# Scans in three parts, pairwise state sums, merged early loads, halved projections and a new order in a two-branch kernel

## The chip, the cores and the metric

The kernel runs on one core of a Trainium2 chip. The metric is device microseconds of one execution. Its engines are TensorE (PE, with its weight loads shown as PEld), VectorE (DVE), ScalarE (ACT), GpSimd (POOL) and SyncE (SP), which issues nearly all DMAs. Each engine takes its instructions strictly in its own program order and waits on semaphores for the others.

## The reference

Two branches on 2048 positions of width 448, all in bf16, joined along the last axis.

```python
# A: attention with 16 heads of 28, each position sees itself and 7 earlier ones, 2 apart
qkv = x @ wqkv;  idx = pos - 2 * arange(8)
logits = einsum("bhsd,bhswd->bhsw", q, k[idx]) * 28 ** -0.5   # -1e9 where idx < 0
o = einsum("bhsw,bhswd->bhsd", softmax(logits), v[idx]);  a = o @ wo
# B: a diagonal complex state space model, 448 states
Lam_bar = exp(exp(log_dt) * Lam);  Bu = x @ (((Lam_bar - 1) / Lam)[:, None] * Bmat).T
h[t] = Lam_bar * h[t - 1] + Bu[t]
b = 2 * real(h @ Cmat.T) + x * Dskip
out = concatenate([a, b], axis=-1)
```

## The kernel before, in words

The program is a list of small steps. ORDER is a string of step names written out by hand or by a planner outside the kernel; the loop at the end calls each step once, in that order, and a step puts its instructions at the end of the queue of the engine that does them. So ORDER alone sets every engine's order, and nothing is rearranged afterwards. In a name such as `QK051`, `QK` is the step and 0, 5, 1 its arguments; `@31` gives the PSUM banks (of eight); a dot at the end makes an eviction an ACT instruction, `=` a DVE one. Steps in capitals are mostly TensorE's, those in small letters the evictions and elementwise work behind them.

**Head.** SP's queue starts with the loads of A's x (`xnA`), of parts of wqkv (`w_load`, 96 KB each in pieces of 128 columns, `w_half` for the last 64 rows), then A's second half, B's x and B. `WU` and `WF` are matmuls of zeros. `XI0`, `XI1`, `XI2` transpose x's first 512 positions on TensorE, `xi..` evict them, `XH1`, `XA10`, `XA11` with `xh1`, `xa..` do the next 512; positions 1024 to 2047 are transposed by DMA (line 183). `PP`, `pcopy`, `pa` to `pg` make the 448 decay rates and tables of constants; `ty`, `tk`, `tf`, `ts` make cosine and sine tables for groups of 64 states (7 groups). POOL fills constants, among them `iot` and `kph`, which `pe` reads.

**Attention.** `QS`(m, s) and `QK`(u, m, k) project q (m even) and k (m odd) of one half u, in four matmuls of 512 columns for the 448 rows of x: three of 128 rows and one of 64. In `QK` and in `V_` (values) and `BU` (B's projection) the 64-row matmuls of two blocks run side by side as one step with last argument 1 (line 259). `qk`, `qh`, `v` evict. `P`(u, r, ws) multiplies q with four shifted k on DVE (line 405, 2048 columns, one of 7 buffers), and `E_`(u, r) sums over the head's rows with matmuls of 32 columns (lines 417, 421); E_06 and E_16 are the last of each half. `lt` evicts logits, `TD` transposes them by DMA, `sma`, `smb`, `smc` are the softmax. `AL`, `al` spread the weights into bands in `Ak` (evictions that need Ak filled with zeros by POOL), `ad` writes them to DRAM and `sp` reads them back skewed into strips `PT` (line 529; PT is first filled with zeros by POOL, `pm0` to `pm2`, line 973; `pm4` fills Ak's second half in the tiles oT and ya, `pm3` wo). `AV`, `av` apply them to the values, `W_`, `w`, `ow` project and store.

**State space.** Time is split into chunks of T = 4 positions, and chunks into even (EV) and odd (OD). `BD` and `xt` are DMA transposes of B and x, `BU` projects, `BR` adds the rotated previous position (line 761), `z` evicts to Z (Z3 for the fourth). `UP` adds even chunks to the odd ones, `y` evicts; the scan runs over odd chunks only. `sa` rotates by table into a real scan, `sb` scans (one instruction a group), `sd` rotates back: in parts of two groups, 0, 2, 4, and group 6 alone, on three work tiles (vv, p2, hs). `DN`(g) and `dn`(g) give the even chunks' states, one group at a time. `H_`, `h` add states to position 0; for positions 1 and 2 `sw` swaps real and imaginary halves by DMA, `hp` multiplies on ACT and `hy`, `hz` add on DVE. `LC`, `ci`, `CD`, `ca`, `cs` load, transpose and scale C. `C`(j, ct), `c`, `oc` give the output, `CH`, `ch`, `oh` the last tile in halves.

`OZ` opens the tiles Z and Z3 in the space of the head's inputs, with a small fill on POOL (line 949) that waits for the last reader of that space, the transposes BD; `OP` opens PT, oT, wo and ya in the space of q, k and C. POOL's order is OZ, pm3, pm4, pm0, pm1, pm2. SP's order behind the head's loads is xt0, TD0, BD0, xt2, xt3, xt1, LC, BD1, TD1, LD, CD3, CD0, CD2, CD1, ad0, ad1, wo, sp0, sp1, ad2 and so on.

Of the kernel before, what the change touches and what calls it, by code (L numbers as in the profile page):

```python
# [63 lines left out]
def kernel(  # L64
# [169 lines left out]
    kph = const.tile([128, 2, 5, G], F32, tag="kph")  # L234
    for k in range(5):
        POOL.memset(kph[:, 0, k], max(k, 1) / (2.0 * T))
    POOL.memset(kph[:, 1], 0.0)
    POOL.memset(kph[64:128, 1, 1:5], 0.25)
# [777 lines left out]
```

## Time and profile before

| | |
|---|---|
| median of 3 executions | 127.11 us (126.85 to 127.17) |
| the profiled execution | 127.13 us |
| its span, first to last instruction | 125.4 us |
| granted TensorE clock | 1.00 |
| instructions | PE 1061, DVE 211, ACT 198, POOL 49 |

All numbers of the prediction come from the profiled execution; what lies around its span is 1.7 us. A row of the timeline has the start in us, the time from the first start to the last end, the engine, the line, the operation with what it writes and reads, the shape and the count, and in square brackets the idle time before it and what ended it. A matmul row is for TensorE, whose instructions overlap: one of 512 columns is shown some 0.38 us long, and the distance of starts tells what it costs. A row of a group has, after the bar, busy us and mean ns of one, then idle us before. A row of stretches has PE, PEld, DVE, ACT and POOL busy time with counts, then the clock, the DMA engines' busy share and GB/s.

### The profile page before, as it was taken

The numbers are of one execution on the slowest core, as the hardware profiler recorded it, in microseconds if no ns is written. First come the engines' busy times: TensorE is split into PE (matmuls) and PEld (weight loads), VectorE is DVE, ScalarE is ACT, GpSimd is POOL, SyncE is SP. The second block draws the span as 40 slices with busy tenths as digits, with TensorE's granted clock in tenths as the row PEclk, the third lists the DMA queues.
The fourth block names the chain that finished last, engine by engine and source line by source line (L and its number), as shares of the span: only waits on it lengthen the run. The fifth ranks groups of instructions, "written<-read, shape, count | busy, mean of one in ns | idle before, by whom it ended". The sixth has DMA issues, their size and how long they took to land.

```text
span 125.4 us, 2898 instructions
## 1 busy us (share of the span) xinstructions
PE 120.6 (96%) x1061; PEld 59.0 (47%) x1061; DVE 113.6 (91%) x211; ACT 102.4 (82%) x198; POOL 22.7 (18%) x49
## 2 busy tenths in 40 slices
PE   6999999999999999999999998999999999999990
...
DVE  4588999899999999999999999999999999998561
ACT  0599899897596999889999999999999999980000
...
GB/s 97 208 278 204 325 251 181 191 194 253 157 143 213 204 204 224 144 127 188 358 221 129 160 154 400 156 100 160 177 130 120 0 169 54 124 103 141 227 180 74
DMA packets 57493, 22.34 MB, mean 178 GB/s; under 512 B 43943, under 2 KB 56935, under 8 KB 57479
## 3 DMA queue, kind: packets, MB, share of 16 engines
...
q10 hardware_dynamic: 207, 0.07, 0.3%
...
## 4 chain that ended last, share of the span: by engine, by line
PE 77%; ACT 17%; DVE 2%; issue 2%; ACTq 0%; DVEq 0%
PE ps L259 27%; PE ps L897 16%; PE ps L573 10%; ACT Z L114 7%; ACT ctmp L722 5%; PE ps L417 5%; PE ps L374 4%; PE ps L560 4%; PE ps L277 2%; PE ps L827 1%; PE ps L375 1%; PE ps L922 1%; PE ps L761 1%; ACT L694 1%; PE ps L421 1%
## 5 line engine op out<-in xcount | busy, mean ns | idle before, releaser
L405 DVE TENSOR_TENSOR pr<-qf,kf 128x2048 bf16<-128x2048 bf16 x24 | 27.9, 1220 | 0.7 <-PE ps L417 0.4
L259 PE MATMUL ps<-xbuf,BT 128*128 128x512 bf16 (+1 forms) x112 | 25.1, 380 | 0.0
L897 PE MATMUL ps<-Cw,Z 128*128 128x448 bf16 x105 | 20.9, 352 | 0.0
L259 PE MATMUL ps<-xT,wq 128*128 128x512 bf16 (+1 forms) x72 | 16.0, 380 | 0.0
L259 PEld LDWEIGHTS <-BT 128*128 128x128 bf16 (+1 forms) x112 | 9.1, 96 | 12.9 <-issue 4.5
L897 PEld LDWEIGHTS <-Z 128*128 128x128 bf16 x105 | 10.3, 98 | 9.5 <-DVE Z L883 0.2
L114 ACT CAST Z<-ps 128x512 bf16<-128x512 f32 (+1 forms) x28 | 13.8, 547 | 0.2
L573 PE MATMUL ps<-wo,oT 128*128 128x448 bf16 x64 | 13.7, 353 | 0.0
L259 PE MATMUL ps<-wq,xT 128*128 128x448 bf16 (+1 forms) x64 | 12.3, 353 | 0.0
L973 POOL MEMSET PT<- 128x4320 f32 x3 | 11.0, 3698 | 4.7 <-DVE z L461 4.7
L259 PEld LDWEIGHTS <-wq 128*128 128x128 bf16 (+1 forms) x72 | 5.9, 97 | 8.6 <-issue 2.4
L722 ACT ACTIVATE ctmp<-Cw,c2t 64x448 f32<-64x448 bf16 x14 | 9.3, 666 | 0.2
L573 PEld LDWEIGHTS <-oT 128*128 128x128 bf16 x64 | 6.2, 98 | 5.7
L259 PEld LDWEIGHTS <-xT 128*128 128x128 bf16 (+1 forms) x64 | 5.2, 97 | 6.8 <-issue 2.4
L114 ACT CAST qf<-ps 128x512 bf16<-128x512 f32 x12 | 6.8, 594 | 1.8 <-PE ps L259 1.5
L114 ACT CAST oT<-ps 128x512 bf16<-128x512 f32 x15 | 8.1, 641 | 0.0
L114 ACT CAST v_s<-ps 128x448 bf16<-128x448 f32 x16 | 7.9, 548 | 0.0
L761 PE MATMUL ps<-Z,R 128*128 128x512 bf16 x21 | 7.3, 381 | 0.5 <-ACT Z L114 0.5
L114 ACT CAST kf<-ps 128x512 bf16<-128x512 f32 x12 | 7.1, 604 | 0.3 <-PE ps L375 0.2
L949 POOL MEMSET Z<- 128x14 bf16 x1 | 0.1, 111 | 38.9 <-ACT Cn L117 38.9
L374 PE MATMUL ps<-xT,wq 128*128 128x512 bf16 x24 | 6.6, 379 | 0.3 <-DVE u L627 0.2
L872 ACT ACTIVATE PT<-PT,bcol 128x512 bf16<-128x512 bf16 x8 | 6.3, 816 | 0.0
...
## 6 DMA issues: line engine op xcount, KB each, us to landing
PT<-pd SPq DMA_DIRECT2D x16, 156.0 KB, 4.8
...
```

Of the source, the lines that this page charges most:

```text
L114: (ACT.copy if e == "A" else V.tensor_copy)(o, i)
L259: PE.matmul(o, l, r, start=(first and i == 0), stop=(not first and i == len(pairs) - 1 and not more[s]))
L374: PE.matmul(p[:], wqk(m, slice(0, 128), kt), xT[:, 0, 4 * s + kt], start=(kt == 0), stop=False)
L405: V.tensor_tensor(t[:], q.unsqueeze(1).to_broadcast((128, 4, 512)), k4, ALU.mult)
L417: PE.matmul(acc[s][32 * i:32 * i + 32], E[:, f, ws, :], t[:, i, :], start=(f == 0 and ws == 0), stop=False)
L560: PE.matmul(p[32 * hh:32 * hh + 32, 128 * bl:128 * bl + n], v_s[:, t, 4 * hg + hh, :], PT[:, t % NS, (4 * hg + hh) // HS, (4 * hg + hh) % ...
L573: PE.matmul(p[:, 0:D], late["oT"][:, b // 4, hg, par, 128 * (b % 4):128 * (b % 4) + 128], late["wo"][:, hg, :], start=(hg == 0), stop=(hg ...
L722: ACT.activation(t[a:a + 64, 0:D], Cw[b:b + 64, g, :], ACTF.Copy, scale=c2t[a:a + 64, g:g + 1])
L761: PE.matmul(pp["z", g, j][:], rot(g, 0), late["Z"][:, g, j - 1, :], start=False, stop=True)
L872: ACT.activation(t, late["SW"][:, NC * g:NC * (g + 1)], ACTF.Copy, scale=bcol[:, j - 1, g:g + 1])
L897: PE.matmul(p[:, 0:D], z, Cw[:, g, :], start=(g == 0), stop=(g == G - 1))
L973: POOL.memset(late["PT"][:, 4 * i:4 * i + 4].rearrange("p t g n -> p (t g n)").bitcast(F32), 0.0)
```

## The change

The scans are done in parts of 2, 3 and 2 groups (0, 2 and 5) on two work tiles: the product that had its own tile goes into hs before the scan and into vv behind it. DN and dn treat groups 0 and 1, 2 and 3, 5 and 6 together in one bank, group 4 alone. The first 256 columns of q and of k are loaded by one DMA each (192 KB) in place of two. A step QA(m, a) projects half of a 512-position block, for m = 0 and 1, in place of QS00 and QS10. POOL fills kph ahead of iot. ORDER is new throughout: which engine evicts what (all four evictions of XI0 and XI1 are DVE's; tk2 to tk6 are ACT's, where all tk were DVE's), the place of every step, and with it the order of each queue. SP's is now LC, TD0, xt2, BD0, xt0, xt1, xt3, LD, CD2, CD0, CD3, TD1, CD1, BD1, ad1, ad0, wo, sp0, sp1, ad2; POOL's is OZ, pm3, pm0, pm1, pm4, pm2, with mz and ab ahead. BU300 stood ahead of E_16 and is now behind it.

```diff
-WU@0 XI0@1 WF0 xi00= xi01= XI2@2 PP@3 pcopy pa XI1@4 WF1 WF2 WF3 xi10. xi20= pb pd_ pc pe xi11. QS00@5 QS10@6 QS30@7
-XH1@0 ty0 ty1 pf tk0= tk1= tf0 XA10@1 xh1= QS20@3 pg ab rb0 ts00 xa10. XA11@2 xa11. QK050@40 qk000. xt0 qk010. P000
-qk020. QS11@1 qk011. P001 mz QS01@2 qk001. qk030. ts10 P010 ts20 ty4 QS21@5 QS31@6 qk031. qk021. QK041@31 tk4= QK051
-P011 V_101@27 QK040 V_100 wj. QK060@65 ty5 qk041. qk040. qk051. v101. V_000@13 qk050. V_011@07 QK061 V_001 v100.
-qh011. P020 E_00@42 v000. v001. P021 E_02 tk5= tf2 qh010. P030 qh001. qh000. E_01 P031 P040 P041 P050 P051 V_010
-V_400@13 hc0 P060 v011. v010. QK110@56 ts02 ts12 V_401 QK101@70 QK111 E_03 P061 qk110. qk111. QK100 qk100. QK120@56
-E_04 qk101. ts22 E_05 E_06 lt00 lt01 QK131@70 QK121 v401. qk120. TD0 QK130 qk130. v400. QK150@42 QK151 QK141@35
-QK161@71 qk131. qk150. P100 P101 P110 qk121. qk151. E_10@03 P111 P120 QK140 qk141. P121 QK160 qk140. V_110@46 V_501@25
-qh110. ty2 V_111 P130 P131 qh111. v110. qh101. qh100. v111. E_11 E_12 V_500 V_410@14 V_510@76 V_411 V_511 ty3 BD0 hc1
-sma0 smb0 E_13 P140 v500. v501. P141 P150 P151 E_14 E_15 v511. v510. xt2 xt3 xt1 BU300@25 v410. v411. P160 P161 LC
-E_16 lt11 BD1 lt10 TD1 smc0 OZ BU301 z30. ci1. LD BU001@67 BU101@14 BU000 ci3. z00. BR31 BU100 BU201@30 z10. AL0@2
-al0. z31. BR01 ci0= CD3 CD0 z01. rb3 tk2= BU200 z20. BR11 z11. dk. ci2= CD2 BU011@61 CD1 OP pm3 AL1@2 BR21 BU010 BR02
-sma1 z21. BU110@57 smb1 z02. ad0 tk3= tf1 ts01 al1= ad1 BU111 BR03 BR12 xd0 BU210@34 z03. pm4 smc1 BU311@02 z12. ts11
-xd1 BU501@65 UP0 BU211 y0= pm0 BR13 BU310 ca3 ca6 z13= wo UP1 cs3 BR32 AX@1 y1= ax. BU500 xd2 ca1 cs6 BU400@71 z50.
-ts21 BR51 BR22 AL2@6 BU401 z32. z22. sp0 BU601@03 BR33 sa0 BR23 al2. ty6 BU600 z33. cs1 UP3 z40. z51. sb0 AL3@6 tk6=
-tf3 BR41 z23. UP2 BU511@75 z60. y3. BU510 BR61 BU411@02 sd0 y2= ca2 ca4 z41. z61. DN0@4 pm1 sp1 BU410 ts03 ad2 BR52
-z52. adx BR42 ts13 z42. BR53 al3= ad3 z53. sa2 dn0 pm2 cs4 AV021@6 av021. AV000@1 AV031@4 AV030@3 UP5 sb2 sd2 av031.
-BR43 z43. sp2 AV010@7 av010= y5= AV011@0 DN1@6 av030. dn1 av011. spx AV001@4 AV020@3 DN2@7 dn2 cs2 hp020 UP4 av020.
-DN3@0 av000. BU610@56 dn3 BU611 BR62 W_10@7 W_20@3 y4= ca5 ca0 av001= z62. sa4 H_01@1 h01 sb4 W_00@0 W_01@2 H_00@4
-hp012 BR63 W_11@5 hp011 w20. w01. ts23 w11. w10. w00. H_03@1 sd4 W_30@3 W_21@2 DN4@5 z63= hp010 h03 UP6 W_31@7 y6. dn4
-hp022 h00 sa6 H_02@0 w21. DN5@1 sp3 AV120@5 av120. dn5 h02 AV111@6 av111. AV131@4 AV121@2 av121. av131. sw2 ow20
-AV101@5 av101. AV100@1 H_04@6 cs5 AV130@0 H_05@2 av130. AV110@4 hp123 av110. av100. w30= W_61@3 W_71@5 hp113 cs0 sb6
-sd6 C32@0 DN6@4 xd3 ow01 hp025 dn6 C33@1 ow11 sw0 hp111 sw4 hp115 hp122 hp112 ow00 H_06@4 h04 w31= ow31 w71= ow10 ow21
-sw6 h05 hp023 hy2 h06 ow30 hp121 C30@6 C31@7 c30 hp021 hz2 hy1 W_51@5 c31 c32 hp124 c33 oc33 C00@2 hp125 C01@4 W_50@6
-oc30 oc32 hp013 hy3 W_60@7 hp114 W_40@0 w61. hz1 hp110 hp120 hy0 hp015 hy5 w51. w50= hz5 hz0 hp024 hp014 hy4 C02@3
-ow71 hp116 hz3 hz4 hp026 hp016 oc31 hp126 hy6 hz6 W_41@1 w41. w60. ow61 ow50 C03@5 c00 oc00 w40. W_70@6 C12@1 C10@7
...
+WU@0 WF0 XI0@1 PP@2 pcopy WF1 WF2 XI2@3 pa WF3 pb pc xi20. xi00= xi01= XI1@4 xi10= xi11= QA00@5 WF4 pe pf pd_ ty1 QA01
+tk1= QS30@6 tk0= QA11@7 QA10 ty0 tf0 qk000. XA10@2 xa10= XH1@1 XA11@3 xh1. QS20@4 xa11. QS01@0 tk4. ts00 QS11@5 qk010.
+wj. qk011. ts10 QS31@1 QK040@23 QS21@7 qk020. QK050@54 pg qk031. qk001. rb0 qk030. qk021. ts20 ty4 QK061@10 QK041 tk5.
+QK051 V_111@67 QK060 qk041. P000 P001 LC P010 P011 P020 P021 ty5 qk051. qk040. V_110 E_00@34 E_02 E_01 qh001. qk050.
+P030 v111. qh000. V_411@25 tf2 P031 P040 v110. ts02 tk3. V_410 QK100@71 v410. QK110@62 qh011. hc0 qh010. P041 QK111
+v411. QK101 QK121@05 qk100. qk101. QK120 qk110. E_03 P050 P051 ts12 P060 qk121. E_05 E_04 qk111. QK131@71 qk120. ts22
+ty2 QK161@65 P061 E_06 lt00 lt01 TD0 QK160 qh101. hc1 xt2 BD0 QK130 xt0 qk130. qk131. P100 P101 P110 P111 P120 P121
+qh110. qh111. xt1 mz qh100. xt3 ci3. P130 QK150@20 QK151 qk151. QK141@34 V_501@71 QK140 qk141. V_500 sma0 ty3 v501.
+V_400@56 E_10@04 E_11 P131 qk140. qk150. P140 P141 P150 v500. ci2. LD CD2 E_12 V_401 V_001@13 v401. V_101@27 v400.
+ci0. V_000 v000. V_100 ci1. V_510@65 v101. V_010@17 CD0 P151 smb0 E_13 P160 CD3 E_15 E_14 v001. v100. V_011 v011.
+V_511 v511. P161 E_16 lt10 smc0 lt11 v010. TD1 BU200@32 BU100@75 rb3 tk2. tf1 ab v510. CD1 dk. xd3 xd1 sma1 BU101
+BU201 BD1 OZ BU001@04 z20. z10. AL1@1 al1. ad1 AL0@6 al0. tk6. ad0 BR21 z21. BU000 z00. BU010@37 BR01 BR11 xd2 ca3 cs3
+z11. BU300@16 z01. smb1 BU301 z30= BU011 BU311@20 BU111@54 BR02 BU110 z02= ts01 BR03 z03. ts11 BR12 z12. ts21 ty6 smc1
+BU401@13 BU400 z40. BR31 BR13 UP0 y0= BU310 z31= z13. tf3 BR41 UP1 y1= OP pm3 wo ca6 AX@5 ax. sa0 pm0 BR32 z32.
+BU210@17 AL2@6 cs6 BR33 z41. ca1 pm1 pm4 al2. BU411@45 z33. ts03 BU211 BR22 sp0 BU410 BR42 AL3@2 z42. sb0 UP3 y3. z22=
+sd0 BR23 z23. al3. ca2 BU600@36 BR43 cs1 UP2 z43= ca4 DN0@1 dn0 BU601 z60. sp1 y2= hp010 BU501@40 pm2 UP4 y4= BU610@21
+sa2 AV021@7 AV031@5 ts13 av021. av031= BR61 z61. BU500 sb2 BU611 ts23 z50. AV011@3 av011. sd2 AV020@7 av020. AV001@6
+av001= AV000@5 av000. hp021 BR51 BR62 ad2 z62. z51. ad3 AV010@4 AV030@3 av030. av010. BU510@75 BU511 adx DN2@2 dn2
+BR52 cs2 DN4@0 BR63 W_01@3 cs4 sp2 z52. BR53 z53= H_00@6 z63. hp011 UP6 dn4 W_20@4 spx UP5 ca5 ca0 W_21@2 W_11@7 w20.
+w01= hp012 sp3 W_10@0 W_31@3 W_00@4 sw0 y5= y6= AV101@5 w11. w10. w00. w21= av101. AV120@1 av120. AV121@2 AV110@7 sa5
+cs0 av110. AV111@0 av111. sb5 AV130@4 ow20 av130. cs5 AV131@5 AV100@1 sd5 hp020 ow01 W_30@7 w30. h00 sw2 av121. av131.
+hp022 hp120 C32@0 DN5@4 w31= dn5 av100. xd0 H_01@7 h01 C30@6 H_02@2 sw5 h02 ow11 H_05@3 h05 hp026 H_03@5 ow00 hp112
+h03 hp110 hy0 H_04@4 hp122 h04 W_40@1 hz0 C33@7 C31@2 hy2 H_06@3 h06 W_70@5 C01@4 c30 hp023 hp024 hp111 hp121 hp014
+hp124 ow31 c31 hp015 oc31 hy1 c32 c33 C00@3 c00 hp114 hp123 hy4 hz2 hz1 oc30 C03@6 hp025 W_71@2 W_61@0 ow10 oc33 hp116
+W_41@7 hp013 hp115 c01 hz4 hp125 hy5 hp113 hy3 w71. W_50@3 W_51@4 ow30 oc32 hz5 w61. hz3 ow21 ow71 ow61 C02@2 hp126
+hp016 hy6 hz6 w51. w50. ow50 W_60@0 C11@4 C10@3 w41= w60. C20@0 w40. ow51 ow40 w70= c02 c03 c10 c11 C12@1 C13@7 c12
+oc00 c13 C21@5 ow60 C22@2 CH0@6 oc03 oc01 ow70 ow41 oc11 oc02 oc12 CH1@3 oc13 c20 c21 oc10 c22 ch0 oc21 oc20 oc22 oh0
...
-    w_load(0, 128, 0, D)
-    w_load(128, 128, 0, D)
+    w_load(0, 256, 0, D)
...
-    POOL.iota(iot[:], [[1, N2]], base=0, channel_multiplier=0, allow_small_or_imprecise_dtypes=True)
...
+    kph = const.tile([128, 2, 5, G], F32, tag="kph")
...
+    POOL.iota(iot[:], [[1, N2]], base=0, channel_multiplier=0, allow_small_or_imprecise_dtypes=True)
...
+    def QA(m, a):
+
+        first = ("qa", m) not in begun
+        begun.add(("qa", m))
+        if first:
+            pp.setdefault(("qk", 0, m), {})[0] = ps()
+        p, c = pp["qk", 0, m][0], slice(256 * a, 256 * a + 256)
+        for kt in range(3):
+            PE.matmul(p[:, c], wqk(m, slice(0, 128), kt), xT[:, 0, kt, c], start=(first and kt == 0), stop=False, skip_group_check=True)
+        PE.matmul(p[:, c], wzz[:, 0, m % 2, 64 * (m - m % 2):64 * (m - m % 2) + 128], xT[:, 0, 3, c], start=False,
+                  stop=(not first), skip_group_check=True)
...
+    SC = {0: 2, 2: 3, 5: 2}
+
     def scan_args(g0):
-        n = 2 if g0 < 6 else 1
+        n = SC[g0]
...
     def sa(g0):
-        pp["scan"] = [late["sc"].tile([128, 2, N2], BF16, tag=n, name=n) for n in ("vv", "p2", "hs")]
-        n, z3, c, si, vv, p2, hs = scan_args(g0)
-        swapped(p2, z3, si)
+        pp["scan"] = [late["sc"].tile([128, 3, N2], BF16, tag=n, name=n) for n in ("vv", "hs")]
+        n, z3, c, si, vv, hs = scan_args(g0)
+        swapped(hs, z3, si)
         V.tensor_tensor(vv, z3, c, ALU.mult)
-        V.tensor_tensor(vv, vv, p2, ALU.add)
+        V.tensor_tensor(vv, vv, hs, ALU.add)
...
     def sd(g0):
-        n, z3, c, si, vv, p2, hs = scan_args(g0)
-        swapped(p2, hs, si)
-        V.tensor_tensor(vv, hs, c, ALU.mult)
-        V.tensor_tensor(z3, vv, p2, ALU.subtract)
+        n, z3, c, si, vv, hs = scan_args(g0)
+        swapped(vv, hs, si)
+        V.tensor_tensor(z3, hs, c, ALU.mult)
+        V.tensor_tensor(z3, z3, vv, ALU.subtract)
+
+    DP = {0: 2, 2: 2, 4: 1, 5: 2}
...
     def DN(g):
         p = pp["dn", g] = ps()
-        PE.matmul(p[:, 0:N2], rot(g, T - 1), late["Z3"][:, g, OD - 1:OD - 1 + N2], start=True, stop=True)
+        for k in range(DP[g]):
+            PE.matmul(p[:, N2 * k:N2 * (k + 1)], rot(g + k, T - 1), late["Z3"][:, g + k, OD - 1:OD - 1 + N2],
+                      start=(k == 0), stop=True, skip_group_check=True)
...
     def dn(g):
-        e = late["Z3"][:, g, EV:EV + N2]
-        V.tensor_tensor(e, pp.pop(("dn", g))[:, 0:N2], e, ALU.add)
+        n = DP[g]
+        e = late["Z3"][:, g:g + n, EV:EV + N2]
+        V.tensor_tensor(e, pp.pop(("dn", g))[:, 0:N2 * n].rearrange("p (g n) -> p g n", g=n), e, ALU.add)
...
     def sw(g0):
-        n = 2 if g0 < 6 else 1
+        n = SC[g0]
```

Left out are the rest of ORDER from the last AV steps on, the lines of kph that move as they are, and `sb`, which only drops p2.

More of the change, by code (lines that the diff above doesn't have):

```diff
@@ L58 @@
-ow71 hp116 hz3 hz4 hp026 hp016 oc31 hp126 hy6 hz6 W_41@1 w41. w60. ow61 ow50 C03@5 c00 oc00 w40. W_70@6 C12@1 C10@7
-C11@0 C13@2 c01 c02 c03 ow41 ow51 oc03 C21@4 oc02 ow40 oc01 w70. C20@6 ow70 c10 c11 c12 oc10 ow60 C22@3 oc11 CH0@5
-CH1@7 oc12 c13 c20 c21 oc13 c22 ch0 ch1 oc20 oc21 oc22 oh0 oh1
+WU@0 WF0 XI0@1 PP@2 pcopy WF1 WF2 XI2@3 pa WF3 pb pc xi20. xi00= xi01= XI1@4 xi10= xi11= QA00@5 WF4 pe pf pd_ ty1 QA01
+tk1= QS30@6 tk0= QA11@7 QA10 ty0 tf0 qk000. XA10@2 xa10= XH1@1 XA11@3 xh1. QS20@4 xa11. QS01@0 tk4. ts00 QS11@5 qk010.
@@ L61 @@
+ch1 oh1
 """
@@ L202 @@
         POOL.memset(col[64:128], hi)
+    kph = const.tile([128, 2, 5, G], F32, tag="kph")
+    for k in range(5):
+        POOL.memset(kph[:, 0, k], max(k, 1) / (2.0 * T))
+    POOL.memset(kph[:, 1], 0.0)
+    POOL.memset(kph[64:128, 1, 1:5], 0.25)
+    POOL.iota(iot[:], [[1, N2]], base=0, channel_multiplier=0, allow_small_or_imprecise_dtypes=True)
     kf = s1.tile([128, 3, HALO + S], BF16, tag="kf")
@@ L232 @@
                        channel_multiplier=-1)
[L234 to L238, printed above, removed]
     wq6 = s2.tile([128, 4, 2, 64], BF16, tag="wq6")
@@ L375, in QS @@
         PE.matmul(p[:], wzz[:, s, m % 2, 64 * (m - m % 2):64 * (m - m % 2) + 128], xT[:, 0, 3], start=False, stop=True)
+    @op
+    def QA(m, a):
[8 more added lines that the diff above has]
+                  stop=(not first), skip_group_check=True)
     @op
@@ L805, in sd @@
     def sd(g0):
-        n, z3, c, si, vv, p2, hs = scan_args(g0)
-        swapped(p2, hs, si)
-        V.tensor_tensor(vv, hs, c, ALU.mult)
-        V.tensor_tensor(z3, vv, p2, ALU.subtract)
+        n, z3, c, si, vv, hs = scan_args(g0)
+        swapped(vv, hs, si)
+        V.tensor_tensor(z3, hs, c, ALU.mult)
+        V.tensor_tensor(z3, z3, vv, ALU.subtract)
+    DP = {0: 2, 2: 2, 4: 1, 5: 2}
     @op
```

2 lines of the change are left out of this document (1 added, 1 removed).

## The prediction

> **What bounds the kernel now.** I read the page first (busy time, the 40 slices, the chain), then the waits, then TensorE's own timeline.
>
> ```profile
> span 125.4 us, 2898 instructions
> PE 120.6 (96%) x1061; PEld 59.0 (47%) x1061; DVE 113.6 (91%) x211; ACT 102.4 (82%) x198; POOL 22.7 (18%) x49
> PE   6999999999999999999999998999999999999990
> DVE  4588999899999999999999999999999999998561
> ACT  0599899897596999889999999999999999980000
> PE 77%; ACT 17%; DVE 2%; issue 2%; ACTq 0%; DVEq 0%
> ```
>
> Three engines are full from 10 to 110 us. The chain gives ACT 17%, all between 53 and 78 us, but a matmul's end is modelled, so busy time cannot say whether TensorE lost anything there. Its starts can.
>
> ```profile
> 22.37 0.35 PE L259 MATMUL ps<-wq,xT 64*128 64x448 bf16 x2
> 22.66 1.48 PE L417 MATMUL ps<-pr,E 128*32 128x512 bf16 x24
> 24.07 2.44 PE L259 MATMUL ps<-wq,xT 128*128 128x448 bf16 x12
> 26.35 1.46 PE L259 MATMUL ps<-xT,wq 128*128 128x512 bf16 x6
> 27.74 0.36 PE L259 MATMUL ps<-wq,xT 64*128 64x448 bf16 x2
> ```
>
> From 24.07 to 26.35 twelve matmuls of 448 columns start 0.190 us apart: no loss. From 26.35 to 27.74 six of 512 columns need 6 x 0.216 = 1.296, and 0.094 is left over, because the next matmul has 64 rows. From 22.37 to 22.66 a side-by-side pair (0.190) and 0.10 more, because the next has 32 columns; from 22.66 to 24.07 six sets of four (1.296) and 0.11. So TensorE goes from start to start without a hole, and pays about 0.095 us at each change of tile shape. Set against these paces, all matmul starts from the first projection on lose few real waits. The largest, in the same view:
>
> ```profile
> 76.72 0.59 PE L761 MATMUL ps<-Z,R 128*128 128x512 bf16 x2
> 77.86 0.38 PE L761 MATMUL ps<-Z,R 128*128 128x512 bf16 x1 [0.54 <-ACT Z L114]
> ```
>
> Two matmuls from 76.72 would let the third start at 77.15; it starts at 77.86, 0.70 lost. Counted like this over all starts, 0.2 goes at 11.2 us, and after 49.87 us 1.7 in all: 0.4 at 69.7, this 0.70, 0.35 among the AV steps, the rest in pieces under 0.1. The kernel is bound by TensorE's order; the other two engines matter where they arrive late.
>
> **The change part by part: the head.**
>
> ```profile
> 3.49 0.82 PE L309 MATMUL ps<-ident,xbuf 128*128 128x128 bf16 x6
> 4.11 0.42 PE L284 MATMUL ps<-wz 128*128 128x128 bf16 x2
> 4.89 0.24 PE L599 MATMUL ps<-ident,raw 7*128 7x7 bf16 x3
> 6.55 0.59 PE L374 MATMUL ps<-xT,wq 128*128 128x512 bf16 x2
> 7.30 0.38 PE L374 MATMUL ps<-xT,wq 128*128 128x512 bf16 x1 [0.16 <-DVE u L627]
> 7.73 0.81 PE L374 MATMUL ps<-xT,wq 128*128 128x512 bf16 x3
> 4.35 0.62 DVE L114 COPY xT<-ps 128x512 bf16<-128x512 bf16 x2 [1.77 <-PE ps L309]
> 6.89 0.36 ACT L114 COPY xT<-ps 128x256 bf16<-128x256 bf16 x1
> ```
>
> QS00 takes 6.55 to 7.73 instead of 4 x 0.216, held by the last eviction of XI1 on ACT (6.89 + 0.36). After, the four evictions of XI0 and XI1 are on DVE behind pcopy and pb, and QA00 and QA01 do QS00's columns by halves. By the rows: WF0 ahead of XI0 puts it at 3.59; PP behind it at 4.37 (its inputs came before 4.89 here); then 4 + 4 + 2 + 6 matmuls at 0.107 end XI1 at 6.25. DVE: pcopy 4.7, pb to 5.5, xi00 and xi01 to 6.05, xi10 from 6.5 (its psum is there 0.35 after the last start, as at 4.35) and xi11 to 7.1. QA01 runs 6.95 to 7.39, and then one projection is done, 0.34 before 7.73. Were DVE held up (below), this could be 0; were XI1 earlier, 0.6. I take 0.34. The eight added halves and two fillers cost nothing more: the fillers stand in a wait, the halves add up to the same columns.
>
> The merged loads of wq shorten packets' total time:
>
> ```profile
> 4.50:5.50 1.00, 1.00 (x13) 0.79 (x11) 0.78 (x4) 0.12 (x1) 0.87 (x5) 1.00 1.07 240
> 7.00:7.50 0.50, 0.34 (x2) 0.10 (x1) 0.40 (x3) 0.50 (x2) 0.00 (x0) 1.00 1.07 365
> ```
>
> With full DMA engines 240 GB/s move while the 256-byte pieces of wq run and 365 with larger ones, so 393 KB take 1.64 us, and 1.08 at best. Between 0 and 0.56 earlier; no step of my sum waits for it, but QK100 now comes 2 us earlier and needs the transposed second half of x, so this gain covers it.
>
> **The order up to E_16.** Steps of 64 rows, E steps and AV steps stand in fewer, longer runs: changes of tile shape fall from 54 to 41, of these from 22 to 19 ahead of E_16 and from 32 to 22 behind it. At 0.095 this is 0.29 and 0.95.
>
> ```profile
> 49.87 0.63 PE L421 MATMUL ps<-pr,E 64*32 64x512 bf16 x16
> 13.08 1.23 DVE L405 TENSOR_TENSOR pr<-qf,kf 128x2048 bf16<-128x2048 bf16 x1
> 46.97 2.35 DVE L405 TENSOR_TENSOR pr<-qh_t,kh 128x2048 bf16<-128x2048 bf16 x2
> 10.34 0.22 DVE L642 TENSOR_TENSOR co<-sc,rk 128x56 f32<-128x56 f32 x1
> 11.89 1.08 DVE L703 TENSOR_TENSOR R<-Is,co 128x896 bf16<-128x896 bf16 x1
> 8.16 1.28 ACT L634 ACT_TABLE_LOAD   x1
> L682 DVE SCALAR_TENSOR_TENSOR kM<-iot,fT,cols 128x256 f32<-128x256 f32 x7 | 3.2, 475 | 0.0
> L405 DVE TENSOR_TENSOR pr<-qf,kf 128x2048 bf16<-128x2048 bf16 x24 | 27.9, 1220 | 0.7 <-PE ps L417 0.4 <-ACT kf L114 0.2
> ```
>
> TensorE is ready for E_16 at 49.87 - 0.34 - 0.29 - 0.2 (the wait at 11.2) - 1.30 (BU300, now behind it) = 47.7. But E_16 needs P161. DVE's chain of products starts at 13.08 here and ends at 49.32. After, the steps ahead of P000 start from xi11's end at 7.1: pe and pd_ take 1.35 at their present spacing, so fT is there at 8.45. On ACT the table load (1.28) begins behind xi20 at 6.55 and pf, ty1 and ty0 follow to 9.5, which tf0 waits for (to 10.2); then xa10 (1024 columns where xh1 has 512, so some 0.2 longer), pg (10.34 to 11.89, 1.55) and rb0 (11.89 to 13.08) put P000 at 13.4. Its factors qk000 and qk010 are evicted by 12.7. Of the 36.24 in between, tk4 and tk5 move to ACT (2 x 0.39 at DVE's spacing) and the waits of 0.6 go: 34.9. P161 ends at 48.3, and TensorE waits 0.6 at E_16. This is what is late next: up to there DVE sets the time.
>
> **Behind E_16.** Here TensorE's remaining 72.61 us (49.87 to its end at 122.48) get BU300 (+1.30), lose 10 changes (-0.95) and the waits of 1.7. What comes in their place:
>
> ```profile
> L787 DVE TENSOR_TENSOR p<-hs,tab 64x512 bf16<-64x512 bf16 x3 | 1.3, 420 | 0.1
> 53.01 0.11 POOL L949 MEMSET Z<- 128x14 bf16 x1 [38.94 <-ACT Cn L117]
> 60.89 10.98 POOL L973 MEMSET PT<- 128x4320 f32 x3 [4.74 <-DVE z L461]
> 45.90 0.59 SPq L289 DMA_DIRECT2D Cr<-in_B_C_im_dram  x1
> 47.08 2.93 SPq L710 DMA_TRANSPOSE BT<-Bn  x1
> 51.68 1.23 SPq L439 DMA_TRANSPOSE attn<-lt  x1
> 53.82 5.23 SPq L715 DMA_TRANSPOSE Cw<-Cn  x4
> 64.62 8.11 SPq L529 DMA_DIRECT2D PT<-pd  x8
> PT<-pd SPq DMA_DIRECT2D x16, 156.0 KB, 4.8
> ```
>
> Scans in three parts: between 512 columns (420 ns) and 2048 (1220) a column costs 0.52 ns, so an instruction 0.15 us beyond its columns, 0.07 when the 0.08 by which DVE's instructions overlap is taken off. Eight instructions fewer give 0.55, three dn fewer 0.2. One work tile less costs nothing: only DVE writes and reads them, in order. It is slack for DVE, not TensorE's time. Adding by pairs makes the first group of a pair wait for the second's product, 0.11 on TensorE; the scan is common already. The five tk that go to ACT cost it about 0.5 each; ACT idles 23 us of the span, but tk2 and tk6 stand at 50 to 54 us, where it is full, so z20 and z10 come up to 0.5 later than they could; the walk below holds them. LC's four loads (some 0.6 of issue each, 2.5 in all) now stand on SP ahead of TD0, which waits for lt01 until 32.4 anyway, and TD0 has till 38 before sma0 needs it. I walked DVE and ACT from each result that TensorE gives them to the next one it needs, adding this trace's spacings in the new order, and set the sum against TensorE's own. In the order of now this shows DVE up to 1.4 late (from y1 on, at AV100) and ACT 1.2 (from al0 on), about the 1.7 seen. In the new order no step comes late by more than 0.2 us, but many are within 0.2 (z02, z31, z22, dn0, hz6): DVE and TensorE run level. Two transfers are also close (next part). New waits behind E_16 lie between 0 and the 1.7 of now; I take 0.4, nearer to the lower end because the walk shows none.
>
> The sum: 48.3 + 72.61 + 1.30 - 0.95 - 1.7 + 0.4 = 119.96 against 122.48, 2.5 less; the profiled execution took 127.13 (0.02 above the median), so **124.6**.
>
> **The rivals.** *TensorE alone:* P000 starts 0.3 earlier and nothing is late behind: 123.9. For it speaks that no single wait stands out; against it that all three engines are at 9 tenths.
>
> *The strips come late.* POOL's order is now the Z3 margin (OZ), pm3, pm0, pm1, pm4, pm2, and OZ waits for BD1, which SP issues behind TD1 and CD1. TD1 follows lt11 at 50.2; 1.2 + 1.3 + 2.9 give 55.7, and between 1.4 and 3.0 to land (here 50.0 to 53.0): OZ at 57.1 to 58.7, pm0 done 4.6 later, sp0's issue at 61.7 to 63.3 (64.62 here), sp1 landing some 11.8 later (7 us of issue and the page's 4.8): 73.5 to 75.1. AV021 comes 25.7 of TensorE's work behind E_16, at 74.0. So 0 to 1.1 lost there, and as much once more at AV101, which needs sp3: 125.6, at most 126.5.
>
> *The array is slow for longer.* The head's 128-column matmuls start 0.107 apart (3.49 to 4.11), QK's 512 columns 0.216 from 6.55, so the pace doubles near 6.4, whatever the clock column says. If that comes 1.5 us later, halves and QS30 cost 1 to 1.5 more, less the 0.6 of slack before E_16: 125.4. The Trainium skill ("TensorE: Matmul & The Clock Gate", Part 1) ties it to a free-running window of about 3.4 us of sustained work. By that it can shift with the phase; here five microseconds pass, and no run yet shows it move.
>
> *Slower:* al2 stands in ACT's order and waits for pm4's first half, which is now behind pm0 and pm1 (3.66 each): OZ + 9.4, so 66.5 to 68.1, against 68.3, when ACT reaches it. From an OZ after 58.9 on, each microsecond holds all of ACT, z's and TensorE behind it. At OZ = 62, with BD1's transfer 3 us later, it would take 127.7.
>
> *No effect:* DVE's level run turns into a bound over the whole second half and the old 1.7 comes back: 126 to 127.1.
>
> **How the numbers follow.** Forecast 0.40 (own range 124.2 to 125.2), TensorE alone 0.20, strips 0.17, slow array 0.07, no effect 0.04, slower 0.12. Within 0.3% of 127.11 is what a measurement of this kernel can't tell from no change. The range from 123.6 to 126.5 holds the first four, less their edges.
>
> **What would show it.** QA01's last matmul near 7.4 and QS30 behind it; P000 at 13.4; a wait of TensorE on DVE's products before E_16 at 48.3; 41 changes at 0.095; TensorE's last start 2.5 earlier. Wrong: TensorE idle at QK100 for the transposed x by more than 0.6; idle before AV021 on sp1; ACT idle before al2 on POOL's fill of oT; projections 0.43 apart after 7 us.

## Result and the profile after

The changed kernel takes 125.23 us (median of 4 executions, 125.22 to 125.26) against 127.11 (126.85 to 127.17): a ratio of 0.985, with a 95% interval of 0.984 to 0.987. It is 1.88 us faster; 2.5 were forecast. The range and the sign hold; the sum is 0.63 too low, and part of its reasons were wrong. One of the executions below was slow (126.00 us at a granted clock of 0.986, in the kernel with BU200 and BU100 in halves) and is left out there.

The page of the changed kernel, its first lines, TensorE's slices and the chain by engine:

```profile
PE 117.3 (95%) x1061; PEld 59.9 (49%) x1071; DVE 112.1 (91%) x198; ACT 103.9 (84%) x200; POOL 22.6 (18%) x49
PE   6995999999999999999999999999999999999990
PE 82%; ACT 11%; DVE 3%; issue 2%; ACTq 0%; DVEq 0%
```

TensorE is busy for 117.3 us where it was for 120.6, and ACT's share of the chain fell from 17% to 11%. Ten matmul records are missing (1061 against 1071 weight loads): they are a part of that smaller busy time, and distances between starts have to be read with the count beside them. One slice stands out, the fourth (9.3 to 12.4 us), half idle. TensorE's timeline in the head, and in the last row one of its weight loads:

```profile
6.81 0.49 PE L385 MATMUL ps<-xT,wq 128*128 128x256 bf16 x3
7.13 0.27 PE L386 MATMUL ps<-xT,wzz 128*128 128x256 bf16 x1
7.55 0.59 PE L373 MATMUL ps<-xT,wq 128*128 128x512 bf16 x2
9.96 0.81 PE L373 MATMUL ps<-xT,wq 128*128 128x512 bf16 x3
12.17 0.38 PE L374 MATMUL ps<-xT,wzz 128*128 128x512 bf16 x1 [1.40 <-ACT xT L114]
7.32 0.33 PEld L373 LDWEIGHTS <-wq 128*128 128x128 bf16 x3 [0.20 <-DMA wq<-in_A_wqkv_dram]
```

QA01's last matmul starts at 7.13 (7.4 was its forecast end). QS30 has three matmuls of 128 rows, and the row at 7.55 shows two: the first has no record. Its weights are loaded at 7.32, 0.20 late for a DMA, and 7.55 less one matmul (0.216) gives 7.33 for its start. Then comes what nothing in the prediction had: QS20's first three matmuls run from 9.96, its fourth starts at 12.17 where 10.61 was due. TensorE stands 1.56 us for ACT's eviction xh1. Behind 12.17 its starts show no hole up to the end beyond the 0.1 of a change of shape, once the nine other missing records are allowed for.

DVE's, ACT's and POOL's timelines at this place, in that order, tell why ACT was late:

```profile
6.87 0.18 DVE L639 TENSOR_TENSOR u<-f,kph 128x35 f32<-128x35 f32 x1
7.16 0.20 DVE L640 TENSOR_TENSOR u<-u,kph 128x35 f32<-128x35 f32 x1
7.39 1.73 DVE L641 TENSOR_SCALAR k<-u 128x35 f32<-128x35 f32 x1
14.75 2.36 DVE L417 TENSOR_TENSOR pr<-qf,kf 128x2048 bf16<-128x2048 bf16 x2
9.38 0.23 ACT L646 ACTIVATE sc<-u 128x35 f32<-128x35 f32 x1 [1.57 <-DVE u L642]
6.85 2.23 POOL L683 MEMSET Ak<- 128x2560 f32 x1
```

The third instruction of `pe`, 35 columns, took 1.73 us; its twin in the kernel before took 0.18, and there POOL filled Ak five microseconds later:

```profile
7.63 0.18 DVE L629 TENSOR_SCALAR k<-u 128x35 f32<-128x35 f32 x1
11.84 2.23 POOL L671 MEMSET Ak<- 128x2560 f32 x1
```

The instruction ends at 9.12, the fill at 9.08. In the new order `mz`, the fill, stands ahead of `ab`, which waits for DVE, so the fill starts as soon as POOL's constants are done. ACT's `pf` then waits 1.57 for DVE, `ty1` and `ty0` and xh1 stand behind `pf`, and P000 starts at 14.75 instead of the 13.4 forecast.

The trace of the kernel before held a small sign of this, under POOL's last constants (DVE's, then POOL's timeline):

```profile
6.11 0.55 DVE L621 TENSOR_SCALAR km<-f 128x7 f32<-128x7 f32 x1
6.51 0.13 POOL L237 MEMSET kph<- 128x35 f32 x1
```

These 7 columns end at 6.66 and POOL's fill of `kph` at 6.64; in the changed kernel, with POOL idle, the same instruction takes 0.16 (at 9.27).

Around E_16 and at the end (DVE's, then TensorE's timeline):

```profile
47.14 2.36 DVE L417 TENSOR_TENSOR pr<-qh_t,kh 128x2048 bf16<-128x2048 bf16 x2
49.21 0.75 PE L433 MATMUL ps<-pr,E 64*32 64x512 bf16 x16
119.03 1.50 PE L941 MATMUL ps<-Cw,Z 128*128 128x224 bf16 x14
```

P161 ends at 49.50 (forecast 48.3); E_16 starts at 49.21, since its first half needs only P160. From there to TensorE's end at 120.53 are 71.32 us, against 72.61 before.

### The profile page after: what moved, and what is told of

Same layout as the page of the kernel before. It is cut to its first block, busy times and chain, and to the rows that moved or that the text cites. A ratio compares the mean times of both kernels' runs of the same rounds, so it can differ in the third digit from the quotient of the medians.

```text
span 123.5 us, 2878 instructions
## 1 busy us (share of the span) xinstructions
PE 117.3 (95%) x1061; PEld 59.9 (49%) x1071; DVE 112.1 (91%) x198; ACT 103.9 (84%) x200; POOL 22.6 (18%) x49
## 4 chain that ended last, share of the span: by engine, by line
PE 82%; ACT 11%; DVE 3%; issue 2%; ACTq 0%; DVEq 0%
PE ps L258 32%; PE ps L916 16%; PE ps L585 10%; PE ps L429 5%; PE ps L572 4%; ACT Z L114 3%; PE ps L773 3%; PE ps L373 2%; PE ps L276 2%; DVE k L641 1%; PE ps L846 1%; PE ps L941 1%; ACT L706 1%; PE ps L374 1%; PE ps L433 1%
## 5 line engine op out<-in xcount | busy, mean ns | idle before, releaser
L258 PE MATMUL ps<-xbuf,BT 128*128 128x512 bf16 (+1 forms) x107 | 23.3, 380 | 0.2
L258 PE MATMUL ps<-xT,wq 128*128 128x512 bf16 (+1 forms) x70 | 15.5, 380 | 0.2 <-issue 0.2
L585 PE MATMUL ps<-wo,oT 128*128 128x448 bf16 x64 | 13.4, 353 | 0.0
L114 ACT CAST Z<-ps 128x512 bf16<-128x512 f32 (+1 forms) x23 | 11.4, 538 | 0.3 <-PE ps L258 0.2
L114 ACT CAST ya<-ps 128x448 bf16<-128x448 f32 (+1 forms) x12 | 6.1, 551 | 0.2 <-PE ps L585 0.2
L926 DVE TENSOR_TENSOR xbuf<-ps,xnB 128x384 bf16<-128x384 f32 x8 | 4.4, 552 | 2.0 <-PE ps L916 2.0
```

Of the source, the lines that this page charges most:

```text
L114: (ACT.copy if e == "A" else V.tensor_copy)(o, i)
L258: PE.matmul(o, l, r, start=(first and i == 0), stop=(not first and i == len(pairs) - 1 and not more[s]))
L585: PE.matmul(p[:, 0:D], late["oT"][:, b // 4, hg, par, 128 * (b % 4):128 * (b % 4) + 128], late["wo"][:, hg, :], start=(hg == 0), stop=(hg ...
L926: V.tensor_tensor(yo[:, 0:384], p[:, 0:384], xP[:, ct, j // 2, 512:896], ALU.add)
```

## Experiments

The theory after the result: (A) POOL's fill holds DVE, and what hangs on it is the 0.6 us missing; (B) rivals, that DVE's long instruction has another cause, or that something else is next in line and would have taken the gain. Beside these, the prices in the sum were tested one by one. All ratios are to the kernel before, timed on the same chip.

### The fill behind `ab`

```diff
-qh110. qh111. xt1 mz qh100. ... tk2. tf1 ab v510.
+qh110. qh111. xt1 qh100. ... tk2. tf1 ab mz v510.
```

> The changed kernel, with POOL's fill of Ak (mz) issued behind ab instead of ahead of it. Theory A, POOL's fill holds up DVE: in the changed kernel the instruction k<-u of pe (line 641) takes 1.73 us, from 7.39 to 9.12, while POOL fills Ak from 6.85 to 9.08; without the fill there it takes 0.2, pe ends at 7.9 in place of 9.35, pf starts at 7.9 instead of 9.38, P000 at 13.2 to 13.5 instead of 14.75, TensorE's wait for xh1 in QS20 (1.56 us from 10.4) shrinks below 0.4, P161 ends near 48.1, and the time is 123.9 to 124.2. Rival B, the long instruction has another cause, such as its operands or the DMAs that run beside it: it stays at 1.7 and the time at 125.2. Rival C, DVE is freed but another input is late next (the second half of x, the evictions of ACT): P000 moves, but the time only to 124.6 to 125.0.

Measured: 125.03 us (124.14 to 125.21), ratio 0.982 (0.980 to 0.985). DVE's, POOL's and TensorE's timelines of this kernel:

```profile
6.99 0.18 DVE L641 TENSOR_SCALAR k<-u 128x35 f32<-128x35 f32 x1
12.05 2.23 POOL L683 MEMSET Ak<- 128x2560 f32 x1
48.09 0.63 PE L433 MATMUL ps<-pr,E 64*32 64x512 bf16 x16
49.76 1.46 PE L258 MATMUL ps<-xbuf,BT 128*128 128x512 bf16 x5 [1.05 <-ACT lt L442]
```

The instruction takes 0.18, and E_16 starts 1.12 us earlier, as theory A has it. But the time hardly moves, as rival C has it: BU200, due at 48.7, starts at 49.76. The profile names ACT's `lt`, but in the changed kernel BU200 starts at 49.89 and `lt` at 50.02, so it doesn't need that. Its other input is the transposed x. What asks for x in this kernel between 43 and 51 us:

```profile
L746 SPq DMA_TRANSPOSE xbuf<-xnB x2: 1617/1876/2134, 42.0 to 43.6; - x2
DMA to landing us min/median/max: 5.9/5.9/5.9
```

The last transpose (xt3) is issued at 43.6 and lands 5.9 later, at 49.5. In the changed kernel it is issued at 43.7 and lands 4.9 later, before TensorE is there. So two things ended last at nearly the same place, and whoever moved one met the other. That it is xt3 which holds BU200 is argued here; the halves below show it.

### The fill early, in the kernel before

```diff
-WU@0 XI0@1 ... P001 mz QS01@2
+WU@0 mz XI0@1 ... P001 QS01@2
```

> The kernel before, with the fill of Ak (mz) as the first of POOL's steps, so that it runs from about 6.8 to 9.05 us as in the changed kernel instead of 11.84 to 14.07. Theory A (the fill holds DVE's instructions with one source): k<-u of pe at 7.63, or already km<-f of pd_ at 6.11, is held until 9.1; P000 starts 1.3 to 2.4 later than 13.08, P161 ends 1.3 to 2.4 later, TensorE reaches E_16 0.7 to 1.9 later, time 127.8 to 129.0. Rival B (another cause in the changed kernel): no long instruction here, 127.1.

Measured: 129.03 us (129.02 to 129.04), ratio 1.015 (1.014 to 1.016). POOL's and DVE's timelines:

```profile
6.84 2.23 POOL L671 MEMSET Ak<- 128x2560 f32 x1
6.95 2.15 DVE L623 TENSOR_SCALAR fT<-fT,cols 128x7 f32<-128x7 f32 x1
7.09 2.01 DVE L627 TENSOR_TENSOR u<-f,kph 128x35 f32<-128x35 f32 x1
```

An instruction of 7 columns lasts from 6.95 to 9.10 and the one behind it as long, though it is a TENSOR_TENSOR; the fill ends at 9.07. Moved alone, the fill costs the kernel before 1.9 us: as much as the whole change won. Theory A holds in both directions.

The Trainium skill ("SBUF — State Buffer", Who interferes with whom) has this: one pair of ports is shared by DVE and GpSimd, `tensor_scalar` can take it in its two-port modes, and whoever comes second is blocked for the whole instruction of the other; a `tensor_tensor` is disturbed only by a GpSimd instruction that reads. The trace agrees for this fill, which only writes: the TENSOR_SCALARs wait to within 0.04 us of its end, and the two TENSOR_TENSORs at 6.87 and 7.16, which overlap it in the changed kernel with no TENSOR_SCALAR ahead of them, take 0.18 and 0.20. Which mode the TENSOR_SCALARs ran in, no run shows.

### The transposes of x: earlier by SP's order

```diff
-    x_load(1)
+    (XL, a step, in ORDER:)  XA11@3 xt0 XL xh1.   # on top of the fill behind ab
```

> The first experiment's kernel (fill of Ak behind ab), and besides SP issues the transpose xt0 behind the loads of B, ahead of the second half of B's x and of TD0, in place of behind TD0 and BD0. Theory: with the fill out of the way E_16 starts at 48.09, 1.12 earlier than in the changed kernel, but BU200 behind it waits 1.2 for the last of the transposed x (xt3 landed at 49.56), and this gave the gain back. With xt0 done in the time in which SP and the DMA engines now wait for lt01 (32 to 34 us), xt3 lands at 46.5 to 48, BU200 starts right behind E_16 at 48.4 to 48.6, and the time is 123.8 to 124.2, with less scatter than the 124.14 to 125.21 of the first experiment. Rival: BU200 waits for something else, or other inputs behind it (smc0, the weights' transpose) come late by as much: 124.8 to 125.1.

Measured: 125.48 us (124.85 to 126.28), ratio 0.987 (0.984 to 0.990): no faster than without it, and rather slower. ACT's and DVE's timelines, from an execution of 126.02 us:

```profile
38.84 0.94 ACT L117 COPY Cn<-Cr 64x896 bf16<-64x896 bf16 x1 [2.56 <-DMA Cr<-in_B_C_im_dram]
39.60 0.29 DVE L456 TENSOR_TENSOR attn<-attn,mk 128x256 bf16<-128x256 bf16 x1 [1.61 <-DMA attn<-lt]
```

xt0 takes its place in SP's queue from LC and TD0; ACT stands 2.56 us at ci3 for C, DVE 1.61 at sma0 for the logits. My theory named the right transfer and the wrong cure: the queue was full, so the earlier transfer only moved the wait.

The same step alone, with the fill left early:

> The changed kernel with xt0 issued early as in the combined version, the fill of Ak left where it is. Theory: up to E_16 the fill sets the time by DVE (P161 ends 49.50) and BU200 doesn't wait for the transposes (xt3 lands at 48.69), so nothing is won: 125.1 to 125.3. Rival: the transposes were the bound already: 124.0 to 124.6.

Measured: 125.75 us (125.21 to 125.96), ratio 0.989 (0.986 to 0.991). Nothing is won, as the theory says; that up to 0.7 is lost it had not, and the cause is probably the same queue.

### BU200 and BU100 in halves

On top of the fill behind ab, and instead of moving a transfer ahead of others, the first use is split, as the change does with QA: the halves of 256 columns that need only xt0 and xt1 come first, and SP issues these two first.

```diff
-hc1 xt2 BD0 QK130 xt0 ... xt1 qh100. xt3 ... E_16 ... BU200@32 BU100@75
+hc1 xt0 BD0 QK130 xt1 ... xt2 qh100. xt3 ... E_16 ... BH200@32 BH100@75 BH201 BH101
+    def BH(g, jp, a):   # columns 256 a to 256 a + 255 of both banks, start only in the first half
```

> The first experiment's kernel (fill of Ak behind ab), and BU200 and BU100 in halves of 256 columns (first halves of both, then second halves), with the transposes in the order xt0, BD0, xt1, xt2, xt3, so that the first halves, 1.3 us of TensorE's work, need only xt0 and xt1. Theory: in the first experiment TensorE stood 1.2 us between E_16 and BU200 for xt3 (landed 49.56 us); with the halves it goes on at 48.4 to 48.7 and meets xt3 at 49.7 to 50.0, so most of that wait is filled: 123.9 to 124.3, and less scatter. Rival: what holds the first experiment's kernel behind E_16 is not xt3 but DVE (smc0, tables) or ACT, which run no earlier: 124.8 to 125.1.

Measured: 124.66 us (124.00 to 124.75, four executions), ratio 0.979 (0.977 to 0.981). TensorE's timeline:

```profile
47.63 0.75 PE L434 MATMUL ps<-pr,E 64*32 64x512 bf16 x16
48.30 2.79 PE L780 MATMUL ps<-xbuf,BT 128*128 128x256 bf16 x24
88.14 0.31 PE L573 MATMUL ps<-PT,v_s 128*32 128x135 bf16 x8 [0.91 <-issue]
```

The halves start right behind E_16, and 24 of them end 2.79 us later, without a hole. That settles what held BU200. Now the next wait shows: TensorE, 1.6 us earlier than in the changed kernel at AV021 (73.50 against 75.10), stands 1.07 at AV101. Its weight loads wait 1.1 for the transfers of sp3. This is the prediction's rival of the strips, at the second place that it named.

### Dskip loaded in the head

```diff
-ci2. LD CD2
+ci2. CD2        # on top of the halves; the load stands in the head, ahead of the transposes of x at 16 us
```

> The kernel with the fill behind ab and the halves of BU200 and BU100, and the load of Dskip (LD, 1.1 us of SP's queue at 45.0) moved to the head, ahead of the transposes of x at 16 us, where SP waits 1.1 us for the second half of x. Theory: in the kernel without this step TensorE, 1.4 earlier than in the changed kernel at AV021, waits 1.07 at AV101 for sp3, the last strip, which hangs on OZ by POOL's fills and the DMA queue, and OZ on BD1 at the end of SP's queue of transposes. With LD gone from there TD1, CD1 and BD1 are issued 0.8 to 1.1 earlier, OZ starts at 56.3 to 56.7 instead of 57.40, sp3 lands 0.7 to 1.1 earlier, and the wait at AV101 falls below 0.4: 123.6 to 124.0. Rival: BD1 lands by the DMA engines' backlog and not by its issue, so OZ stays near 57.4 and the time at 124.6.

Measured: **123.83 us** (123.60 to 124.12), ratio 0.975 (0.973 to 0.977), the fastest of all and 1.4 below the changed kernel. POOL's OZ in the kernel without and with this edit, and TensorE's rows at AV101 and at the end with it:

```profile
57.40 0.11 POOL L983 MEMSET Z<- 128x14 bf16 x1 [43.13 <-DMA BT<-Bn]
```

```profile
56.61 0.11 POOL L980 MEMSET Z<- 128x14 bf16 x1 [42.34 <-ACT ctmp L736]
86.92 0.42 PE L574 MATMUL ps<-PT,v_s 128*32 128x135 bf16 x16
87.17 0.18 PE L568 MATMUL ps<-PT,v_s 128*32 128x7 bf16 x4
117.42 1.50 PE L953 MATMUL ps<-Cw,Z 128*128 128x224 bf16 x14
```

One short load less in SP's queue lets BD1 be issued at 52.68 in place of 53.47, and brings OZ forward by the same 0.79 us (the profile names ACT for its wait in the second row, but OZ has moved exactly as BD1 did); the wait at AV101 is gone.

The same kernel with the fill early again, for the fill's share:

> The last kernel (halves of BU200 and BU100, Dskip loaded in the head) but with POOL's fill of Ak ahead of ab again, as in the changed kernel. Theory: up to E_16 the fill sets the time by DVE's k<-u (1.7 us again, P161 ends near 49.5), and the transposes and strips are not late without it, so the two other edits bring nothing alone: 125.1 to 125.4. Rival: the other edits carry the gain of 1.4 and the fill is hidden: 123.8 to 124.2.

Measured: 125.22 us (125.21 to 125.26), ratio 0.985 (0.983 to 0.987), E_16 at 49.21 as in the changed kernel. So the fill costs 1.39 us (125.22 - 123.83, on two chips where the kernel before takes 127.12 and 127.11) once the transposes and strips don't take its place, and those two edits are worth nothing while it stands.

### The price of a change of tile shape

```diff
-BU200@32 BU100@75 ... BU101 BU201
+BU200@32 BU201 BU100@75 ... BU101     # likewise BU011, BU211 and BU601
```

> The changed kernel, with four steps of 64 rows behind E_16 (BU201, BU011, BU211, BU601) taken out of their runs and put right behind their projections' 128-row parts: eight more changes of tile shape, the same work, nothing asked for earlier than it is ready. By the price of my sum, 0.095 us at each, the time is 0.76 longer: 125.9 to 126.0, and TensorE's starts show eight gaps of 0.095 more. Rival: a change costs nothing by itself, the 0.095 belongs to the weight loads or to psum and is paid anyway: 125.2.

Measured: 126.25 us (126.24 to 126.26), ratio 0.993 (0.992 to 0.994): 1.02 longer for eight changes. TensorE's timeline of the changed kernel at BU601, and of this one:

```profile
73.02 0.60 PE L258 MATMUL ps<-xbuf,BT 64*128 64x512 bf16 x4
73.55 0.28 PE L785 MATMUL ps<-Z,R 128*128 128x256 bf16 x1
73.67 1.49 PE L258 MATMUL ps<-xbuf,BT 128*128 128x512 bf16 x6
75.10 0.69 PE L572 MATMUL ps<-PT,v_s 128*32 128x135 bf16 x32
```

```profile
74.09 0.39 PE L258 MATMUL ps<-xbuf,BT 64*128 64x512 bf16 x2
74.41 0.28 PE L785 MATMUL ps<-Z,R 128*128 128x256 bf16 x1
74.53 1.65 PE L258 MATMUL ps<-xbuf,BT 128*128 128x512 bf16 x6
76.11 0.61 PE L572 MATMUL ps<-PT,v_s 128*32 128x135 bf16 x26
```

Two side-by-side pairs in a run cost 0.53 and one alone 0.32, so two apart cost 0.64: 0.106 more (before rounding) for the second change back to 128 rows. A moved step adds a change at either end, 0.21, and the four together 0.85. Most of the other 0.17 is a wait: BU610 takes 1.58 (74.53 to 76.11) where it took 1.43, because TensorE stands inside it for `dn0` on DVE, which empties its bank until 74.88. The rival, no cost by itself, is out. The Trainium skill ("TensorEngine Tiling (Array Packing)", Key Properties) says that a change of the tiling mode drains TensorE, and gives no figure; that each change costs something here, 0.106, agrees.

### The scan in four parts

```diff
-    SC = {0: 2, 2: 3, 5: 2}
+    SC = {0: 2, 2: 2, 4: 1, 5: 2}    # sa4 sb4 sd4 behind sd2, sw4 behind sw2
```

> The changed kernel with its scan of three groups (2, 3, 4) split into two parts, groups 2 and 3 and then group 4 alone, one behind the other on the two work tiles: eight more DVE instructions of 0.07 each beyond their columns, and two DMAs more. Theory: this work lies in DVE's slack, DVE's part grows by 0.5 to 0.6 and the time by at most 0.2: 125.2 to 125.4. Rival: DVE and TensorE run level there and the whole is paid: 125.8.

Measured: 126.75 us (126.72 to 126.77), ratio 0.997 (0.995 to 0.998): 1.5 longer, beyond both the theory and its rival. DVE's timeline of the changed kernel in the three-group part, and DVE's and TensorE's of this one:

```profile
74.57 0.55 DVE L801 TENSOR_TENSOR hs<-Z,tab 64x768 bf16<-64x768 bf16 x1
75.14 0.55 DVE L802 TENSOR_TENSOR hs<-Z,tab 64x768 bf16<-64x768 bf16 x1
```

```profile
79.94 0.28 DVE L801 TENSOR_TENSOR hs<-Z,tab 64x256 bf16<-64x256 bf16 x1
80.23 0.29 DVE L802 TENSOR_TENSOR hs<-Z,tab 64x256 bf16<-64x256 bf16 x1
80.55 0.29 DVE L809 TENSOR_TENSOR vv<-Z,tab 128x256 bf16<-128x256 bf16 x1
80.88 0.29 DVE L810 TENSOR_TENSOR vv<-vv,hs 128x256 bf16<-128x256 bf16 x1
83.20 0.27 PE L831 MATMUL ps<-Z,R 128*128 128x256 bf16 x1 [0.92 <-DVE Z L823]
```

These instructions don't overlap: they start 0.29 apart for 256 columns and 0.57 for 768, so one has 0.15 beside its columns, and 0.04 more goes where one needs the one before (80.55 to 80.88). The same groups take 1.6 us longer on DVE in two parts (sd ends at 83.15, and at 81.54 in the changed kernel), 0.2 for each of the eight instructions, not 0.07. And hardly any of it is slack: in the changed kernel TensorE needs sd2 at 81.67, 0.13 after its end, so here it stands 1.08 at DN4 and 0.28 at W_01 behind it.

### Three smaller parts undone

The states of even chunks added one group at a time:

```diff
-        V.tensor_tensor(e, p[:, 0:N2 * n]..., e, ALU.add)
+        for k in range(DP[g]): V.tensor_tensor(e, p[:, N2 * k:N2 * (k + 1)], e, ALU.add)
```

> The changed kernel, with the even chunks' states added one group at a time on DVE again (dn as instructions of 256 columns; TensorE's part of the pairs stays): three instructions more. The prediction gave 0.2 on DVE for them and called it slack. By the two rows of such instructions (0.75 for two of 256, 0.69 for one of 512) 0.08 each, 0.24 in all. Where the four-part scan was paid in full, DVE ran level with TensorE from sd2 to dn5, so I expect about the third of it that stands there: 125.2 to 125.5. Rival: dn depends on nothing that is late, and nothing is paid: 125.2.

Measured: 125.34 us (125.33 to 125.35), ratio 0.986 (0.984 to 0.987): 0.11 longer, inside the expectation. Behind E_16 TensorE takes 71.40 us where it took 71.32, so 0.08 of it is seen there, about a third of the 0.24 expected on DVE; the rest is within what two chips differ (the kernel before takes 127.15 on this one).

Whole projections for the halves, and the small loads of wqkv:

```diff
-QA00@5 WF4 pe pf pd_ ty1 QA01 tk1= QS30@6 tk0= QA11@7 QA10
+QS00@5 WF4 pe pf pd_ ty1 tk1= QS30@6 tk0= QS10@7
```

> The changed kernel, with whole projections QS00 and QS10 in the places of QA00 and QA10, and no halves. The prediction gave the halves 0.34 on TensorE in the head. In the changed kernel P000 waits for the chain of pe, pf, ty, tf0, pg and rb0, and TensorE for xh1 on ACT behind the same chain, so the head of TensorE has 1.5 to spare: QS30 comes 0.2 to 0.5 later, P000 stays at 14.75 and the time at 125.1 to 125.4. Rival: the halves bring their 0.34 through to the end: 125.6.

```diff
-    w_load(0, 256, 0, D)
+    w_load(0, 128, 0, D)
+    w_load(128, 128, 0, D)
```

> The changed kernel, with the first 256 columns of q and k loaded by two DMAs of 128 columns each again. The prediction gave the larger loads 0 to 0.56 and no step of its sum. QS30, the first to use columns of k, starts 0.3 later than QA01 lets it in the changed kernel (7.55 against 7.24), so it may come another 0.3 to 0.6 later, inside the same 1.5 to spare; later loads on SP's queue move by two issues, some 1.0, to the transposes of x, which have about 1 to spare ahead of BU200. Time 125.2 to 125.5. Rival: SP's queue has no room for two issues more and the x transposes hold BU200: 125.8 to 126.3.

Measured: 125.30 us (125.21 to 126.68, three of the four up to 125.39), ratio 0.988 (0.984 to 0.992), and 125.33 (125.30 to 125.36), ratio 0.986 (0.984 to 0.987). TensorE's timeline of the first, then of the second:

```profile
7.28 0.81 PE L373 MATMUL ps<-xT,wq 128*128 128x512 bf16 x3
12.18 0.38 PE L374 MATMUL ps<-xT,wzz 128*128 128x512 bf16 x1 [1.47 <-ACT xT L114]
```

```profile
7.22 0.81 PE L374 MATMUL ps<-xT,wq 128*128 128x512 bf16 x3
12.18 0.38 PE L375 MATMUL ps<-xT,wzz 128*128 128x512 bf16 x1 [1.30 <-ACT xT L114]
```

In both QS30 starts no later than in the changed kernel (7.28 and 7.22 against 7.33; the 7.55 in the expectation was the row with a record missing), and in both TensorE then waits for xh1 until 12.18. The differences are within what one head shows: in the kernel of the single sums, which has the changed kernel's, QS30 starts at 7.40. Neither part brings anything here.

## Why the prediction was right and where it was wrong

- **TensorE's order is the bound, without holes, and a change of shape costs 0.095.** Right. Behind 12.17 us the changed kernel's TensorE loses nothing but the changes of shape, 41 of them as forecast, and the price measured apart is 0.106.
- **The head: halves bring 0.34.** The number holds and the cause doesn't. One projection is done at 7.24 (7.39 forecast), and the next starts at 7.33, 0.40 before 7.73. But with whole projections QS30 comes no later, so the halves are not what brings it. And the gain is lost again at QS20. That XI1's evictions are all on DVE and done before 7 us is probably what does it; no run put them back.
- **P000 at 13.4.** This is the step that failed: 14.75. The walk of DVE's chain took its spacings from the kernel before, in which POOL was idle while `pe` ran. `mz` moved ahead of `ab` on POOL, and the prediction gave this no cost. The rest of the walk to P161 holds: from P000's start to P161's end 34.75 measured, 34.9 forecast. Yet with P000 at 13.10, in the first experiment, the kernel still takes 125.03: the walk behind E_16, in which no step came late by more than 0.2, had no term for xt3 at BU200, 1.1 us there and hidden behind the fill in the changed kernel.
- **TensorE waits 0.6 at E_16 for P161.** It is some 0.1 (the 16 matmuls of E_16 take 0.75, and 0.63 in the first experiment). TensorE was as late itself (1.56 at QS20, from the same cause), and E_16 needs P161 only for its second half. Against the forecast P161 costs 1.2 and this gives 0.3 back.
- **Behind E_16: 71.66, with 0.4 for new waits.** 71.32: with BU300, the changes and the old waits as summed, 0.06 is left for new waits. So the sum's error is 1.2 - 0.3 - 0.34 = 0.57 on TensorE's end, of the 0.63 in the time. Half of the 1.2 was made up by errors the other way; that the total came so near is luck to that extent.
- **Scans in three parts are slack for DVE, 0.55.** Wrong twice: a split part costs 1.6, and nearly all of it reaches the end (1.52). The 0.07 took off an overlap of 0.08 that these instructions don't have; the trace before shows two of 512 columns start 0.44 apart (78.85 and 79.29) and last 0.42. The sum had no term of its own for the scans, so it wasn't hurt; that they don't matter to TensorE was wrong. Of the pairs of dn some 0.1 is paid, about half of the 0.2 that was called slack.
- **The strips.** OZ came at 58.19, inside the 57.1 to 58.7 given, and AV021 didn't wait. The rival became real when TensorE was 1.6 earlier, at AV101.
- **al2 on ACT, the slower case.** ACT reached al2 at 69.49, and POOL had filled its tile by 67.46: a margin of 2.0 us.
- **The array slow for longer.** Not seen: three starts of 256 columns from 6.81 to 7.13 are 0.107 apart, the full pace.
- **TensorE alone, 123.9.** It was refused because three engines were at 9 tenths. With the fill moved, BU200 and BU100 in halves and Dskip's load out of the way the kernel does run at 123.83: E_16 starts at 47.63 (47.7 was TensorE's own time in the sum), and 71.30 follow.

What stays open: what brings the head's first projections forward, and why the executions of some kernels scatter (the first experiment's lie 1.1 us apart, the changed kernel's 0.04). That the early fill hides a scatter of the transfers is likely, and not shown.
